# Projection products as four 32-column tiles between score visits that hold a value sum

## The chip, the core and the metric

The kernel runs on one core of one Trainium2 chip. The metric is the device time of one execution in microseconds (us). The core has a matrix engine (TensorE, PE in the profile; its weight loads are listed as PEld), a vector engine (VectorE, DVE), a scalar engine (ScalarE, ACT), a general engine (GpSimd, POOL) and an engine that here only issues DMAs (SyncE, SP). TensorE writes to PSUM, a memory of banks of 128 partitions x 512 float32.

## The reference

Two attention layers over 2,048 tokens, model width 640, 32 heads of 20, bfloat16; their outputs stand side by side.

```
A (memory-augmented, 4 segments of L = 512):
  q, k, v = x @ wq, x @ wk, x @ wv             per head, per segment s
  a_dot = softmax(q k^T / sqrt(20) + mask) v   inside the segment; the mask adds -1e9 where key > query
  a_mem = phi(q) M / (phi(q) z + 1e-6)         phi(t) = t + 1 if t > 0 else exp(t)
  o     = g * a_mem + (1 - g) * a_dot          g = sigmoid(beta) per head
  M    += phi(k)^T v ;  z += sum phi(k)        after the segment
  out_A = o @ wo
B (sliding window of 256):
  q, k, v = x @ wqkv
  out_B = softmax(q k^T / sqrt(20), where 0 <= query - key < 256) v @ wo
out = concat(out_A, out_B)
```

## The kernel before

The work is cut into eight chunks of 512 tokens that alternate, A0, B0, A1, B1 and so on to B3. For each chunk TensorE does three kinds of work, and each kind uses its array in another way, called a mode here:

- **Scores** (`score_batch`, line 745): four heads at once, each on 20 rows of the array (mode "row", or "row64" where only 64 keys are taken). One such batch is a *score visit*; there are 153. A visit fills two score tiles (`sc`, three buffers of two PSUM banks); ScalarE turns each into probabilities by an exponential (`pt`, line 761), and GpSimd (line 800) or VectorE (line 778) masks them.
- **Value sums** (`av`, line 814, and `av_tile`, line 835, for the last chunk): probabilities times values, four heads at once, each on 32 columns of the array and 32 PSUM partitions (mode "col"). Afterwards VectorE transposes (line 870) and GpSimd normalises (line 905).
- **Products** (`wide`, line 857): the q, k and v projections, the output projections, and the memory read `mem`, all on the whole array (mode "full"). There are 1,073 of them; most are part of a sum of five into one of the two PSUM banks `m0` and `m1`, which VectorE then copies out (lines 488, 664, 1014).

Nothing is scheduled on the chip: the order of all engines is written out while the kernel is built. `body` walks a planner's clock (`Flow`): `f.pe`, `f.act` and so on are the times at which the planner thinks each engine is free, and `on_pe` adds 97 ns whenever the mode changes. At each step `body` tries, in this order, a score visit (if its buffers and its q and k are there, and `may_wait` does not put it off), then the first entry of the list `pend` of due value sums and memory reads, then the first job that is ready among `jobs` (projections of the next chunk) and `fins` (output projections). A job yields between matmuls, so score visits may fall inside a sum of five. When all visits are out (`all_scored`), output projections use the score tiles instead of `m0` and `m1`, and the copy out of PSUM goes to ScalarE or VectorE, whichever the planner thinks is free; `last_job` and `last_half` finish the last 128 tokens.

`may_wait` is where `LEAD` acts:

```
if f.pe + LEAD > f.act:
    return False
```

It answers whether a score visit that could go may be put off; `f.act` is the planned end of ScalarE's queue.

`room` holds a score visit of 64-key tiles or a value sum back where many matmuls were issued in the last 3,000 planned ns; `on_pe` books each matmul for it through its argument `n`.

Of the kernel before, what the change touches and what calls it, by code (L numbers as in the profile page):

```python
# [13 lines left out]
P = 128  # L14
# [3 lines left out]
HD = 32  # L18
# [32 lines left out]
PATIENCE = 5000.0  # L51
LANES = 8
AHEAD = 100.0
LEAD = 500.0

def at_head(h):
    return VS * h + 12 * (h // 16)
# [1 line left out]
def mm_ns(n):  # L59
    return max(27.0, n / 2.4 + 2.5)  # L60

def whole(times):

    got = [t for ts in times for t in ts]
    return None if None in got else max(got)
# [147 lines left out]
class _K:  # L213
# [27 lines left out]
        self.f.bank_free[i] = t  # L241

    def warm_up(self, z):

        f = self.f
        ps, bi = self.bank()
        f.pe = max(f.pe, 1500.0)
        while f.pe + 700.0 < max(self.done[(0, "x", 0)], self.done[("wk_A", 0)]):
            self.wide(ps, z[:, 0:P], z[:, 0:L], L, True, True)
            f.flush()  # L250
        self.close(bi, f.seen)
# [602 lines left out]

    def wide(self, ps, lhsT, rhs, n, start, stop):

        self.nc.tensor.matmul(ps[:, 0:n], lhsT=lhsT, rhs=rhs, start=start, stop=stop)  # L857
        self.f.on_pe("full", mm_ns(n), n)
        self.f.left = 0 if stop else self.KT - 1 if start else self.f.left - 1

    def turn(self, O, bi):

        f = self.f
        while self.ring("tt", NTT) is None:
            if f.idle_dve:
                f.idle_dve.pop(0)[1]()
            else:
                heapq.heappop(f.later)[2]()
        tt, slot = self.piece("tt", NTT, 1, F32)
        self.nc.vector.transpose(out=tt[:], in_=O[:, :])  # L870
        t = f.on_dve(640.0, max(f.seen, slot["free"]))
        self.close(bi, t)
        return tt, slot, t
# [279 lines left out]
    def may_wait(self):  # L1153


        f = self.f
        if f.pe + LEAD > f.act:
            return False
# [56 lines left out]
    def body(self, xA, A_wq, A_wk, A_wv, A_wo, A_beta, xB, B_wqkv, B_wo, out2d):  # L1215
        nc, D, KT, f = self.nc, self.D, self.KT, self.f
# [89 lines left out]
        for m in range(KT):  # L1306
            first("k", m, self.kA, pk0)
            first("q", m, self.qA, None)
            v = lambda half: self.v_job(0, half, self.wv_A, self.vA, True,
                                        [self.known(0, "x"), self.known("wv_A", half)])  # L1310
# [5 lines left out]

        bs = self.batches(chunks)
        free_after = {}
        pend = []
        parts = {}  # L1320
        left = {}
        o_t = {}
        groups_done = {n: 0 for n in range(NC)}
# [3 lines left out]
        while True:  # L1327
# [3 lines left out]
            if i < len(bs):  # L1331
                n, ent, ms, complete = bs[i]
                kind, c = chunks[n]
                if self.ring("pt", NPT) is not None:
# [4 lines left out]
                    if None not in need:  # L1339
                        t = max(need + [f.room(4 * len(ent)) if ent[0][1][0] in "lust" else 0.0])  # L1340
# [21 lines left out]
            if pend:  # L1362
                n, g, what = pend[0]
                kind, c = chunks[n]
                if what == "tile":
                    ps_ = [p for x in range(4) for p in parts[(n, g[1] + x)]
                           if p[1] // P == g[0]]
                    need = [whole(p[6] for p in ps_), self.done.get((n, "v", g[1]))]
                elif what == "av":
                    ps_ = parts[(n, g)]  # L1370
# [4 lines left out]
                if None not in need and not (f.open and 0 < f.left <= 3):  # L1375
                    t = max(need + [min(f.bank_free), f.room(
                        4 * len(ps_)) if what != "mem" else 0.0])
# [9 lines left out]
            for x, jb in enumerate(self.jobs + self.fins):  # L1387
                if f.open and not jb[0] is self.opener:
                    continue
                t = self.need_time(jb[1])  # L1390
# [191 lines left out]
```

## Time and profile before

| what | before |
|---|---|
| median of 3 runs | 334.92 us (334.56 to 336.06) |
| profiled execution, time | 334.66 us |
| profiled execution, span | 332.9 us |
| TensorE busy | 317.7 us (95%), 6,617 matmuls and as many weight loads |
| ScalarE busy | 302.4 us (91%) |
| VectorE / GpSimd busy | 266.0 us (80%) / 255.7 us (77%) |
| granted TensorE clock | 1.00 |
| instruction queue q8 | 51 packets, 0.84 MB |

The span runs from the first to the last instruction of the program; the execution's own time lies 1.76 us above it. Busy times are unions of the recorded instructions of an engine. Matmuls are pipelined and the ends of their records are modelled, so a record of 300 ns can stand 137 ns behind the one before it; how long a product occupies the array is read from the distance of the starts. In a list of waits, "issue" means that an engine waited for nothing that the profile shows.

### The profile page before, as it was taken

The numbers are of one execution on the slowest core, as the hardware profiler recorded it, in microseconds if no ns is written. First come the engines' busy times: TensorE is split into PE (matmuls) and PEld (weight loads), VectorE is DVE, ScalarE is ACT, GpSimd is POOL, SyncE is SP. The second block draws the span as 40 slices with busy tenths as digits, with TensorE's granted clock in tenths as the row PEclk, the third lists the DMA queues.
The fourth block names the chain that finished last, engine by engine and source line by source line (L and its number), as shares of the span: only waits on it lengthen the run. The fifth ranks groups of instructions, "written<-read, shape, count | busy, mean of one in ns | idle before, by whom it ended". The sixth has DMA issues, their size and how long they took to land.

```text
span 332.9 us, 15825 instructions
## 1 busy us (share of the span) xinstructions
PE 317.7 (95%) x6617; PEld 174.1 (52%) x6617; DVE 266.0 (80%) x556; ACT 302.4 (91%) x332; POOL 255.7 (77%) x648
## 2 busy tenths in 40 slices
PE   7999999999999999999999999999999999999996
PEld 2444446554444455546654546455654545666564
DVE  6878667788988899989958898888677898876653
ACT  1879999998999999999999999989999999999841
POOL 8446779987668799984876879996965969977750
PEclk9999999999999999999999999999999999999999
DMA  6975745846566852245699245044584054659762
GB/s 195 397 245 135 194 134 121 177 117 183 127 207 145 182 147 75 47 98 107 167 209 189 65 90 161 2 98 69 136 168 114 14 161 126 154 135 192 169 138 99
DMA packets 76260, 47.36 MB, mean 142 GB/s; under 512 B 48381, under 2 KB 73181, under 8 KB 76189
## 3 DMA queue, kind: packets, MB, share of 16 engines
q1 hardware_dynamic: 75469, 45.71, 56.2%
q8 instruction: 51, 0.84, 1.0%
q10 hardware_dynamic: 720, 0.66, 0.7%
q14 instruction: 20, 0.16, 0.2%
HBM read 17.62 MB, written 16.96 MB: 104 GB/s over the span
## 4 chain that ended last, share of the span: by engine, by line
PE 56%; DVE 16%; ACT 11%; POOL 7%; issue 6%; DMA 2%; SPq 1%; ACTq 0%; DVEq 0%; POOLq 0%
PE m L857 35%; PE sc L745 11%; ACT pt L761 11%; PE m L814 6%; POOL pt L800 4%; DVE pt L778 3%; PE m L835 2%; POOL u L905 2%; DVE tt L870 2%; DVE kA L488 2%; DVE pq L529 2%; DMA beta<-in_A_beta_dram 1%; DVE vA L664 1%; DVE pq L523 1%; DVE ot L1014 1%
## 5 line engine op out<-in xcount | busy, mean ns | idle before, releaser
L761 ACT ACTIVATE pt<-sc 128x1024 bf16<-128x1024 f32 (+2 forms) x306 | 284.8, 1014 | 12.4 <-PE sc L745 10.0
L800 POOL TENSOR_SCALAR_AFFINE_SELECT pt<-pt 128x128 bf16<-128x128 bf16 (+1 forms) x512 | 176.7, 373 | 62.1 <-ACT pt L761 58.4
L870 DVE STREAM_TRANSPOSE tt<-m 128x512 f32<-128x512 f32 x88 | 61.4, 711 | 20.3 <-PE m L814 9.6
L905 POOL TENSOR_TENSOR o<-tt,rr 128x320 bf16<-128x320 f32 x64 | 47.6, 743 | 4.4 <-DVE rr L895 4.1
L857 PEld LDWEIGHTS <-xT 128*128 128x128 bf16 x350 | 32.0, 97 | 25.0 <-issue 13.3
L745 PE MATMUL sc<-qB,kB 20*64 20x64 bf16 (+2 forms) x1728 | 38.6, 218 | 1.2 <-issue 0.7
L778 DVE TENSOR_TENSOR pt<-pt,ends 128x1024 bf16<-128x1024 bf16 (+2 forms) x50 | 36.0, 734 | 0.0
L745 PEld LDWEIGHTS <-kB 20*64 20x64 bf16 (+1 forms) x1728 | 21.6, 98 | 23.3 <-issue 22.0
L745 PE MATMUL sc<-qA,kA 20*64 20x64 bf16 (+4 forms) x1024 | 33.3, 237 | 0.4 <-ACT qA L485 0.2
L1014 DVE CAST ot<-m 128x320 bf16<-128x320 f32 x56 | 26.8, 485 | 7.5 <-PE m L857 7.3
L857 PEld LDWEIGHTS <-oT 128*128 128x128 bf16 x280 | 24.7, 98 | 11.4 <-issue 1.0
L857 PE MATMUL m<-wBv,xT 128*128 128x320 bf16 x160 | 27.0, 299 | 2.4 <-DVE tt L870 2.3
L857 PE MATMUL m<-wv_A,xT 128*128 128x320 bf16 x160 | 26.1, 299 | 2.6 <-DVE vA L664 1.9
L857 PE MATMUL m<-xT,wq_A 128*128 128x512 bf16 x100 | 25.8, 380 | 1.5 <-DVE vA L664 1.0
L857 PE MATMUL m<-xT,wk_A 128*128 128x512 bf16 x100 | 26.0, 388 | 1.1 <-DVE qA L488 0.7
L857 PE MATMUL m<-xT,wBq 128*128 128x512 bf16 x100 | 26.8, 381 | 0.1
L857 PE MATMUL m<-xT,wBk 128*128 128x512 bf16 x100 | 25.9, 381 | 0.0
L745 PEld LDWEIGHTS <-kA 20*128 20x128 bf16 (+1 forms) x1024 | 13.6, 97 | 20.8 <-issue 19.8
L814 PE MATMUL m<-pt,vA 128*32 128x192 bf16 (+3 forms) x512 | 23.7, 275 | 0.0
L857 PE MATMUL m<-wo_A,oT 128*128 128x320 bf16 x140 | 22.7, 300 | 0.2
L488 DVE CAST kB<-m 128x512 bf16<-128x512 f32 x20 | 13.8, 691 | 9.2 <-PE m L857 9.2
L857 PE MATMUL m<-wo_B,oT 128*128 128x320 bf16 x120 | 19.4, 300 | 0.3 <-DVE ot L1014 0.3
(108 smaller groups left out, 405.9 us busy)
## 6 DMA issues: line engine op xcount, KB each, us to landing
out_dram<-ot SPq DMA_DIRECT2D x29, 160.0 KB
scr_o<-o SPq DMA_DIRECT2D x28, 160.0 KB
xT<-in_B_x_dram SPq DMA_DIRECT2D x8, 288.0 KB
xT<-in_A_x_dram SPq DMA_DIRECT2D x8, 256.0 KB
scr_pk<-e SPq DMA_DIRECT2D x15, 128.0 KB
vS<-vA SPq DMA_DIRECT2D x16, 87.0 KB
vL<-vB SPq DMA_DIRECT2D x8, 174.0 KB
scr_kA<-kA SPq DMA_DIRECT2D x16, 60.0 KB
```

What stands on the lines that cost most here:

```text
L488: nc.vector.tensor_copy(out=dst[:, m, at:at + L], in_=ps[:, :])
L529: nc.vector.tensor_tensor(out=r if len(box) == 1 else e, in0=r, in1=e, op=ALU.min)
L745: nc.tensor.matmul(ps[j // 2][h0:h1, j % 2, c0:c0 + nq], lhsT=k[rows, g, k0:k0 + h1 - h0], rhs=q[rows, g, q0:q0 + nq], start=True, stop=Tr ...
L761: nc.scalar.activation(out=pt[:, :, lo:hi], in_=ps[i][:, :, lo:hi], func=ACT.Exp, scale=self.scale)
L778: nc.vector.tensor_tensor(out=blk, in0=blk, in1=self.ends[:, c0, :].unsqueeze(1).unsqueeze(1) .to_broadcast([P, 2, n // SH, SH]), op=ALU.mult)
L800: nc.gpsimd.affine_select(out=blk, in_=blk, pattern=pat, compare_op=ALU.is_ge, fill=self.zero, base=base, channel_multiplier=mul)
L814: nc.tensor.matmul(O[HD * j:HD * j + HD, q0:q0 + nq], lhsT=v[:, at_head(h):at_head(h) + HD], rhs=pts[j // 2][:, j % 2, c0:c0 + nq], start= ...
L835: nc.tensor.matmul(O[HD * j:HD * j + HD, o0:o0 + nq], lhsT=v[:, at_head(h):at_head(h) + HD], rhs=pts[j // 2][:, j % 2, c0:c0 + nq], start= ...
L857: self.nc.tensor.matmul(ps[:, 0:n], lhsT=lhsT, rhs=rhs, start=start, stop=stop)
L870: self.nc.vector.transpose(out=tt[:], in_=O[:, :])
L905: nc.gpsimd.tensor_tensor(out=to[:] if add_to else to, in0=a, in1=b, op=ALU.mult)
L1014: nc.vector.tensor_copy(out=ot[:, 320 * hf:320 * hf + 320], in_=ps[:, 0:320])
```

## The change

`wide` now has two forms. In the new one a product is written as four matmuls on 32 columns each, in the mode of the value sums, and the planner books the mode "col" for it. It is taken in two cases: the planner's mode is already "col" and the next due value sum is not of the last chunk (or none is due); or the mode is not "full" and a value sum falls due soon (`sums_soon`: within the first `PEEK` = 2 entries of `pend`, memory reads skipped, a value sum whose probabilities and values are planned to be there within `SOON` = 700 ns; none for the last chunk). Otherwise the product goes over the whole array as before. `LEAD` goes from 500 to 800. `pend` and `parts` become attributes so that `wide` can see them.

```diff
-LEAD = 500.0
+LEAD = 800.0
+COL_NS = 3.0
+SOON = 700.0
+PEEK = 2
...
     def wide(self, ps, lhsT, rhs, n, start, stop):
 
-        self.nc.tensor.matmul(ps[:, 0:n], lhsT=lhsT, rhs=rhs, start=start, stop=stop)
-        self.f.on_pe("full", mm_ns(n), n)
+        f = self.f
+        if f.mode == "col" and not (self.pend and self.pend[0][0] == len(self.chunks) - 1) or f.mode != "full" and self.sums_soon():
+            for j in range(4):
+                s = slice(HD * j, HD * j + HD)
+                self.nc.tensor.matmul(ps[s, 0:n], lhsT=lhsT[:, s], rhs=rhs, start=start,
+                                      stop=stop, tile_position=(0, HD * j),
+                                      skip_group_check=True)
+            f.on_pe("col", n / 2.4 + COL_NS, n, 0.0, 4)
+        else:
+            self.nc.tensor.matmul(ps[:, 0:n], lhsT=lhsT, rhs=rhs, start=start, stop=stop,
+                                  skip_group_check=True)
+            f.on_pe("full", mm_ns(n), n)
         self.f.left = 0 if stop else self.KT - 1 if start else self.f.left - 1
+
+    def sums_soon(self):
+
+        f = self.f
+        if self.pend and self.pend[0][0] == len(self.chunks) - 1:
+            return False
+        for n, g, what in self.pend[:PEEK]:
+            if what == "mem":
+                continue
+            t = self.sums_need(n, g, what)
+            return t is not None and t <= f.pe + SOON
+        return False
+
+    def sums_need(self, n, g, what):
+        if what == "tile":
+            ps_ = [p for x in range(4) for p in self.parts[(n, g[1] + x)] if p[1] // P == g[0]]
+            t = self.done.get((n, "v", g[1]))
+        else:
+            ps_ = self.parts[(n, g)]
+            t = self.done.get((n, "v", g))
+        t0 = whole(p[6] for p in ps_)
+        return None if t is None or t0 is None else max(t, t0)
...
-        pend = []
-        parts = {}
+        self.pend = pend = []
+        self.parts = parts = {}
```

The prediction speaks of the order of the built program: the list of each engine's instructions as the kernel writes them out, which can be read without running it.

More of the change, by code (lines that the diff above doesn't have):

```diff
@@ L243, in warm_up @@
     def warm_up(self, z):
+        self.pend = []
         f = self.f
```

## The prediction

> **What bounds the kernel now.** I read the page's busy times first, then the waits, then the busy time of each engine by chunk, then TensorE's timeline around single changes of array mode. From the page, each engine's busy time:
>
> ```profile
> PE 317.7 (95%) x6617; PEld 174.1 (52%) x6617; DVE 266.0 (80%) x556; ACT 302.4 (91%) x332; POOL 255.7 (77%) x648
> ```
>
> TensorE (PE) leads, ScalarE (ACT) is close. A busy PE includes the modelled ends of matmuls, so the share alone does not say which of the two sets the pace. The waits (engine and line, what it waited for: us in total, times, longest):
>
> ```profile
> PEld L745 <- issue: 41.8, 131, 0.9
> PEld L857 <- issue: 32.3, 121, 1.0
> ACT pt L761 <- PE sc L745: 10.0, 24, 1.5
> ```
>
> The first two are not waits for data: the next weight load sits behind a change between score, product and value-sum modes. The third is ACT starved of scores: 10.0 us in 24 places. Then stretches, each from one chunk's first score visit to the next chunk's, the last row after the final visit (length; busy time of PE, PEld, DVE, ACT, POOL with instruction counts; clock; DMA share; GB/s):
>
> ```profile
> 8.40:47.60 39.20, 38.43 (x597) 18.37 (x600) 29.20 (x59) 35.75 (x41) 22.65 (x70) 1.00 0.71 215
> 47.60:89.20 41.60, 39.97 (x881) 22.26 (x874) 34.19 (x68) 39.73 (x48) 35.34 (x82) 1.00 0.61 155
> 89.20:123.40 34.20, 33.35 (x621) 16.21 (x619) 29.34 (x69) 33.74 (x37) 27.35 (x76) 1.00 0.68 163
> 123.40:167.80 44.40, 42.25 (x982) 25.11 (x981) 40.66 (x83) 42.66 (x48) 37.34 (x81) 1.00 0.44 108
> 167.80:202.20 34.40, 33.54 (x633) 16.51 (x631) 27.95 (x64) 33.83 (x36) 26.68 (x76) 1.00 0.69 135
> 202.20:245.00 42.80, 40.88 (x972) 23.92 (x971) 35.18 (x71) 40.57 (x45) 36.93 (x81) 1.00 0.44 96
> 245.00:279.20 34.20, 33.36 (x633) 16.37 (x631) 28.04 (x64) 33.73 (x36) 26.55 (x76) 1.00 0.43 115
> 279.20:317.10 37.90, 36.63 (x1065) 24.34 (x1063) 28.70 (x62) 36.10 (x40) 31.24 (x74) 1.00 0.71 157
> 317.10:332.90 15.80, 12.61 (x235) 8.79 (x234) 7.38 (x15) 4.56 (x7) 4.43 (x10) 1.00 0.44 114
> ```
>
> ACT's idle time (length less ACT) is 3.45, 1.87, 0.46, 1.74, 0.57, 2.23, 0.47 and 1.80 us: 12.6 us before the final visit. In A chunks 2, 4 and 6 ACT is full, so a lighter PE gains little there. After the final visit PE works alone.
>
> **The price of a mode change.** TensorE's timeline (start us, us, engine, line, shape, count, idle):
>
> ```profile
> 308.91 1.53 PE L857 MATMUL m<-wo_B,oT 128*128 128x320 bf16 x10
> 310.38 0.40 PE L745 MATMUL sc<-qB,kB 20*128 20x128 bf16 x16
> 310.71 0.30 PE L835 MATMUL m<-pt,vB 128*32 128x128 bf16 x8
> ...
> 102.16 0.59 PE L814 MATMUL m<-pt,vA 128*32 128x448 bf16 x12
> 102.58 0.29 PE L814 MATMUL m<-pt,vS 128*32 128x64 bf16 x16
> 102.69 0.21 PE L814 MATMUL m<-pt,vA 128*32 128x64 bf16 x4
> ```
>
> Ten 320-column products last 1.53 us with a single one at 0.30 (page: 300 ns), so one starts every (1.53 - 0.30)/9 = 0.137 us, and the tenth stops streaming at 308.91 + 1.37 = 310.28. The score matmuls start at 310.38: 0.10 us lost. Those 16 go four at a time, four steps of about 0.055 us, done at 310.60; the value sums start at 310.71: 0.11 us. I take 97 ns a change, bounds 90 and 110.
>
> **The change, part by part.**
>
> *Fewer changes.* In the built order TensorE changes mode 382 times before and 324 times after; score visits stay at 153. Of the 62 stretches between visits that hold a value sum, 51 are now in column mode throughout. 58 x 97 ns = 5.6 us less on PE (5.2 to 6.4).
>
> *273 of 1,073 products as four tiles.* A product becomes four loads and four matmuls, 819 more of each. Its streaming time: the twelve 448-, 320- and 192-column matmuls (three steps, four at a time) fill 102.16 to 102.58, 0.42 us for 960 columns, or 0.44 ns a column; the product above has 0.137/320 = 0.43. So column mode streams at the same rate, and I take nothing for the 273. The trace has no product in this mode, so I keep the 0.01 ns between the two as the bound: 0.01 x 380 columns (their mean, about) x 273 = 1.0 us either way.
>
> The four loads must hide. The sixteen 64-column matmuls start at 102.58 and the next group at 102.69: 0.11 us for four steps, each with four loads of mean 96 ns (row of L814's loads), 28 ns a step. So loads overlap the steps before them. [...]
>
> *More instructions to fetch.* The page's instruction queue q8 moved 51 packets, 0.84 MB (16 KB each), which fits TensorE's 13,234 loads and matmuls at 63 bytes; 1,638 more add 12%. What a shortage costs is seen perhaps once: eleven score matmuls at 315.41 stand 0.74 us behind "issue" after a burst of 64. I take nothing, bounds 0 and 4.7 us (6.4 more packets, 0.74 us each).
>
> *LEAD 500 to 800.* `may_wait` puts a score off only if ACT's queue reaches beyond `pe + LEAD`; a larger LEAD puts scores off less. The order shows it: products ahead of the final score visit fall from 174.9 to 169.8 us of streaming, and those behind it rise from 9.6 to 14.7. So 5.1 us move into the last stretch, where only PE works and is hardly idle until 329.8: all 5.1 us (0.6 either way) lengthen the tail. The short description of the change says the opposite of what the test does.
>
> *Moved copies.* Four more 640-column copies go from VectorE (DVE, two of 485 ns) to ACT, in the tail, where ACT is busy 4.56 of 15.80 us. Each takes about 0.69 us beside 1.37 us of products; nothing. Four output stores and some DMA issues swap queue with them; they land beside work, except the last one, which ends the span as now.
>
> *What is late next.* Before the final visit PE has 10.7 us less to do (5.6 + 5.1). It can bring that visit forward only as far as ACT has idle time to give. By chunk, PE's work in the order (columns plus 97 ns a change) falls by 0.7, 2.1, 1.6, 0.3, 2.1, 0.9, 2.1 and 0.9 us. Taking the smaller of that and ACT's idle: 0.7 + 1.9 + 0.5 + 0.3 + 0.6 + 0.9 + 0.5 + 0.9 = 6.3. Chunks 2, 4 and 6 leave 4 us unused; PE may carry a lead over into the next chunk, but three score tiles hold only half a visit beyond the one being read, about one exponential (1,014 ns). So 0 to 1 us at each of three borders; I take half, 1.5. Sum: 7.8 us (6.3 to 9.3).
>
> Total: 5.1 - 7.8 = -2.7, less nothing else. The profiled execution took 334.66 us (span 332.9, 1.76 around it), giving 332.0; the median shown, 334.92, is 0.26 above it. I round the gain to 2.5: **332.4 us**. A measurement of this kernel can tell about 0.5% (1.7 us) from no change.
>
> **Rivals.**
>
> 1. *PE alone sets the end* (0.18). 95% busy speaks for it, the full ACT in chunks 2, 4 and 6 against. All 5.6 us show: 329.3.
> 2. *ACT cannot come earlier* (0.22), slower. In the B chunks its idle may end with a query or key copied by DVE (busy 40.66 of 44.40 us in chunk 3), not with a freer PE. Then LEAD has moved 5.1 us into the tail and gets less back. It decides below 5.1 us of ACT idle recovered; at 3 us the time is 334.9 + 2.1 = 337.0. For it: the smallest fall in PE work is where DVE is fullest. Against: the waits name PE for 10.0 us of ACT's idle.
> 3. *Instruction fetch* (0.07): 4.7 us of stalls against a gain of 2.5, 337.1. Against: stretches of 64 score matmuls and value sums already run denser than any product in four tiles.
> 4. *Loads do not hide* (0.03): one load (97 ns) exposed per product, 273 x 97 ns = 26.5 us, about 359. The 28 ns step speaks against.
> 5. *It does not do what it says*: the mode changes do go (order), the "put off" does not; that is already in the sum.
>
> **How the numbers follow.** The forecast case (0.50) spans ACT recovering 6 to 9.3 us: 334.0 to 330.7. About 0.3 of it lies over 1.7 us below today, 0.2 within. Rival 1 adds 0.18 to faster; rival 2 gives 0.16 to slower and 0.06 to same; rival 3 splits 0.06 to slower and 0.01 to same; rival 4 is slower. Faster 0.48, same 0.27, slower 0.25. The range runs from rival 1 (329.3, less 0.3 for the upper price of a change) to rival 2's 337.0, leaving out rival 4 and the far side of rivals 2 and 3.
>
> **What would show it.** After: "issue" waits of the weight loads down by about 58 places; four-tile products of 320 columns starting 0.137 us apart; ACT's wait for scores down from 10.0 us to some 3 to 4; the final score visit near 309.3 instead of 317.15; then 17 to 18 us of tail in place of 12.6 of PE work. If the final visit is later than 312, rival 2 holds; if the 320-column step exceeds 0.15 us, rival 4; new "issue" gaps within a mode, rival 3. A time outside 329 to 337 would make the sum wrong altogether.

## The result, and the profile after

The changed kernel takes 339.88 us (median of 17 runs, 336.21 to 341.62); before takes 334.68 (17 runs, 333.98 to 336.06). The ratio is 1.0138, 95% interval 1.0115 to 1.0161: **slower by 1.4%**, where 0.7% faster was forecast. (The ratio compares the mean times, without the run of 341.62 us, which fell in a slower state of the chip.) The profiled execution took 339.30 us, span 337.6, against 334.66 and 332.9: 4.6 to 4.7 us longer.

Busy times of the engines, page of the changed kernel:

```profile
PE 313.6 (93%) x7401; PEld 177.7 (53%) x7436; DVE 263.8 (78%) x548; ACT 301.3 (89%) x336; POOL 254.8 (75%) x648
```

TensorE (PE) is less busy than before (313.6 against 317.7 us) in a longer span. (35 matmul records are missing here; each can look like a short gap.) The waits:

```profile
PEld L750 <- issue: 42.7, 127, 1.3
PEld L871 <- issue: 24.0, 76, 1.9
PEld L866 <- issue: 11.6, 46, 1.1
ACT pt L766 <- PE sc L750: 11.6, 22, 1.7
PE sc L750 <- issue: 2.7, 2, 1.5
PE m L819 <- POOL pt L805: 2.0, 3, 0.7
```

ScalarE (ACT) is starved of scores for 11.6 us, not less than the 10.0 before. The last two lines are new in size: score matmuls stopped behind no data for 2.7 us (0.7 before), and value sums waited 2.0 us for GpSimd's masks. Then the same stretches as in the prediction, from one chunk's first score visit to the next, the last one after the final visit:

```profile
8.00:47.80 39.80, 37.63 (x675) 19.06 (x684) 29.51 (x59) 35.62 (x42) 23.58 (x71) 1.00 0.69 213
47.80:87.80 40.00, 37.53 (x931) 21.90 (x933) 33.35 (x64) 38.45 (x46) 34.13 (x81) 1.00 0.59 154
87.80:122.00 34.20, 31.70 (x687) 16.07 (x683) 29.55 (x68) 33.63 (x38) 26.73 (x75) 1.00 0.71 152
122.00:166.90 44.90, 41.84 (x1072) 25.90 (x1071) 40.11 (x84) 42.49 (x48) 37.61 (x81) 1.00 0.48 122
166.90:201.30 34.40, 31.79 (x696) 15.68 (x695) 27.19 (x61) 32.87 (x37) 26.77 (x77) 1.00 0.56 118
201.30:243.90 42.60, 40.05 (x1049) 23.94 (x1050) 35.16 (x70) 40.49 (x44) 36.60 (x80) 1.00 0.38 88
243.90:276.70 32.80, 31.61 (x698) 15.60 (x695) 27.57 (x61) 32.79 (x37) 26.89 (x77) 1.00 0.44 103
276.70:315.80 39.10, 36.87 (x1087) 24.01 (x1080) 28.29 (x60) 35.76 (x39) 31.09 (x73) 1.00 0.75 163
315.80:337.60 21.80, 18.23 (x544) 13.37 (x542) 7.81 (x16) 7.62 (x12) 4.58 (x10) 1.00 0.51 137
```

Two rows carry the loss. The last stretch is 21.8 us instead of 15.8, with 18.23 us of PE instead of 12.61: the products that LEAD moved. (Its border lies 0.36 us ahead of the final visit here; from the visit itself it is 21.4 us against 15.8.) The stretches before it hardly shrank: the last chunk begins 2.5 us earlier (276.7 against 279.2), then takes 39.1 us instead of 37.9, so the final visit comes only 1.0 us earlier (316.16 against 317.15). ACT's idle before it, length less ACT over the first eight rows, is 15.7 us instead of 12.6. The trace of this execution has no record of the granted clock, so the 1.00 in its rows is not measured; but nowhere in it do products of 320 columns follow each other 0.27 us apart, as they do inside the half-clock window of the run with tiles alone below.

The last chunk loses its lead at one place. Its second score visit starts 2.2 us earlier than before (279.18 against 281.38), its third only 0.7 us (282.21 against 282.88). In both kernels a value sum and a product of the memory read stand between these two visits; in the changed order seven output products have come in as well, and they wait for a transpose:

```profile
281.15 1.14 PE L866 MATMUL m<-wo_A,oT 128*32 128x320 bf16 x28 [0.34 <-DVE tt L907]
282.21 1.29 PE L750 MATMUL sc<-qB,kB 20*64 20x64 bf16 x64
```

ScalarE then idles for 1.70 us, its longest wait for scores in this execution.

A product in four tiles costs what was forecast. TensorE's timeline, ten products of 320 columns as 40 matmuls:

```profile
320.50 1.53 PE L866 MATMUL sc<-wo_B,oT 128*32 128x320 bf16 x40
321.86 1.12 PE L866 MATMUL sc<-wo_A,oT 128*32 128x320 bf16 x28
```

(1.53 - 0.30)/9 = 0.137 us apart, the same as on the whole array, and the next group starts 1.36 us on. Counted in the trace, mode changes are 382 before and 324 after. Two stalls stand out, both inside one mode:

```profile
172.89 0.39 PE L750 MATMUL sc<-qA,kA 20*128 20x448 bf16 x7
174.81 0.18 PE L750 MATMUL sc<-qA,kA 20*128 20x64 bf16 x1 [1.52 <-issue]
...
313.10 0.23 PE L750 MATMUL sc<-qB,kB 20*128 20x128 bf16 x4
314.49 0.35 PE L750 MATMUL sc<-qB,kB 20*128 20x128 bf16 x12 [1.15 <-issue]
```

Score matmuls that wait for no semaphore start 1.52 and 1.15 us late. The DMA records have a 16 KB packet of the instruction queue q8 landing 1.43 and 1.52 us before (at 173.37 and 312.97). In the kernel before, the one such stall (0.74 us, at 315.41) ended 1.33 us after a packet (314.08).

### The profile page after: what moved, and what is told of

The parts are those of the page before. It is cut to its first block, busy times and chain, and to the rows that moved or that the text cites. A ratio compares the mean times of both kernels' runs of the same rounds, so it can differ in the third digit from the quotient of the medians.

```text
span 337.6 us, 17420 instructions
## 1 busy us (share of the span) xinstructions
PE 313.6 (93%) x7401; PEld 177.7 (53%) x7436; DVE 263.8 (78%) x548; ACT 301.3 (89%) x336; POOL 254.8 (75%) x648
## 4 chain that ended last, share of the span: by engine, by line
PE 30%; DVE 11%; ACT 6%; issue 5%; POOL 2%; DMA 2%; SPq 1%; ACTq 0%; DVEq 0%; POOLq 0%
PE m L871 12%; ACT pt L766 6%; PE sc L750 5%; PE m L866 5%; PE m L819 3%; DVE tt L907 3%; PE sc L866 2%; PE m L840 2%; POOL pt L805 2%; DVE pt L783 1%; DMA qB<-scr_qB 1%; DVE ot L1051 1%; DVE pq L534 1%; DVE kA L493 1%; DVE qB L493 1%
## 5 line engine op out<-in xcount | busy, mean ns | idle before, releaser
L766 ACT ACTIVATE pt<-sc 128x1024 bf16<-128x1024 f32 (+2 forms) x306 | 281.3, 1034 | 14.2 <-PE sc L750 11.6
L783 DVE TENSOR_TENSOR pt<-pt,ends 128x1024 bf16<-128x1024 bf16 (+2 forms) x50 | 37.9, 767 | 0.0
L871 PEld LDWEIGHTS <-xT 128*128 128x128 bf16 x275 | 24.9, 97 | 18.9 <-issue 8.9
L1051 DVE CAST ot<-m 128x320 bf16<-128x320 f32 x48 | 23.3, 485 | 11.4 <-PE m L871 8.3
L871 PE MATMUL m<-wBv,xT 128*128 128x320 bf16 x135 | 21.9, 299 | 1.2 <-DVE vB L674 0.6
L871 PEld LDWEIGHTS <-oT 128*128 128x128 bf16 x198 | 17.2, 98 | 8.7 <-issue 1.1
L871 PE MATMUL m<-xT,wBk 128*128 128x512 bf16 x72 | 20.4, 380 | 1.2 <-issue 0.6
L871 PE MATMUL m<-xT,wq_A 128*128 128x512 bf16 x67 | 18.1, 380 | 1.5 <-DVE vA L669 0.5
L493 DVE CAST qB<-m 128x512 bf16<-128x512 f32 x20 | 13.8, 689 | 7.2 <-PE m L866 6.6
L674 DVE CAST vB<-m 128x320 bf16<-128x320 f32 x32 | 15.1, 472 | 4.1 <-PE m L866 1.6
L942 POOL TENSOR_TENSOR u<-tt,rr 128x320 bf16<-128x320 f32 x24 | 17.4, 724 | 0.4 <-DVE rr L930 0.4
```

Source lines behind the costliest of these rows:

```text
L493: nc.vector.tensor_copy(out=dst[:, m, at:at + L], in_=ps[:, :])
L674: nc.vector.tensor_copy(out=dst, in_=src)
L766: nc.scalar.activation(out=pt[:, :, lo:hi], in_=ps[i][:, :, lo:hi], func=ACT.Exp, scale=self.scale)
L783: nc.vector.tensor_tensor(out=blk, in0=blk, in1=self.ends[:, c0, :].unsqueeze(1).unsqueeze(1) .to_broadcast([P, 2, n // SH, SH]), op=ALU.mult)
L942: nc.gpsimd.tensor_tensor(out=to[:] if add_to else to, in0=a, in1=b, op=ALU.mult)
L1051: nc.vector.tensor_copy(out=ot[:, 320 * hf:320 * hf + 320], in_=ps[:, 0:320])
```

## The experiments

All are compared with before on the same chip, five rounds; the ratios are not those of the medians and can differ from them by a few tenths of a per cent. The expectations name theories T1 to T4, each explained where it first comes up. The three columns on the right come from one profiled execution of each kernel. "Lead at the last chunk" is how much earlier than before the first score visit of chunk B3 (the 134th) starts in the profiled execution; "final visit" likewise (+ is later); "tail" runs from the start of the final visit to the end of the last product's columns. "Quartered" products shift the places where instruction packets end (see below).

| kernel | ratio (95%) | lead at the last chunk, us | final visit, us | tail, us |
|---|---|---|---|---|
| before | 1 | 0 | 0 | 12.5 |
| changed | 1.0138 (1.0115 to 1.0161) | 2.5 | -1.0 | 18.1 |
| LEAD 800 alone | 1.0125 (1.0085 to 1.0165) | 5.9 | -3.2 | 19.1 |
| changed, LEAD 500 | 1.0308 (1.0286 to 1.0330) | -6.3 | +11.5 | 12.0 |
| tiles on the order of before | 1.0001 (0.9973 to 1.0030) | 2.5 | +0.4 | 12.5 |
| order of the changed kernel, whole products | 1.0209 (1.0183 to 1.0234) | 1.8 | +2.7 | 17.6 |
| tiles on the order of before, 21 quartered | 0.9995 (0.9973 to 1.0017) | 0.9 | -0.7 | 12.5 |
| before, 21 quartered | 1.0088 (1.0059 to 1.0117) | -1.6 | +4.2 | 12.5 |
| changed, LEAD 650 | 1.0136 (1.0101 to 1.0171) | 2.8 | +4.6 | 12.1 |
| LEAD 800 order, tiles | 1.0117 (1.0087 to 1.0147) | 4.6 | -1.8 | 18.7 |
| tiles on the order of before, 10 quartered | 0.9951 (0.9930 to 0.9971) | -0.5 | +0.1 | 12.5 |
| tiles on the order of before, 32 quartered | 0.9999 (0.9974 to 1.0024) | 0.0 | +2.6 | 12.5 |
| changed, 21 quartered | 1.0154 (1.0128 to 1.0180) | 3.0 | +1.3 | 18.5 |
| LEAD 800 alone, 21 quartered | 1.0127 (1.0093 to 1.0160) | | | |

**LEAD alone.** The kernel before with one constant changed:

```diff
-LEAD = 500.0
+LEAD = 800.0
```

> The kernel before with LEAD 800 instead of 500 and nothing else: no product in tiles. Its order on TensorE has 393 mode changes (before 382), and the products behind the last score visit rise from 9.6 to 16.0 us of streaming. Theory T1 (the 5 to 6 us that LEAD moves into the tail are the loss, because ScalarE cannot come forward): 4 to 6 us slower, last score visit about where it was. Theory T2 (the extra weight loads and matmuls run TensorE out of instructions, and scores come late): within 1.5 us of before, since it has no extra instruction. Theory T3 (a product in tiles costs more than a whole one): as before, within 1.5 us.

1.0125, T1's number; T2's and T3's "within 1.5 us" missed. The tail grew by 6.6 us, and the visits, 5.9 us ahead at the last chunk, kept 3.2 us at the end. The third visit of that chunk loses 1.6 us of the lead, as in the changed kernel (five output products stand ahead of it here). Then comes:

```profile
291.00 0.58 PE L857 MATMUL m<-wo_A,oT 128*128 128x320 bf16 x3 [1.98 <-issue]
```

with TensorE's clock at half from 291.6 to 295.0 us. So the tail (T1) is paid, but T1 was wrong that ScalarE cannot come forward: it came 5.9 us forward, and T2's stall appeared in a kernel without one extra instruction.

**Tiles with LEAD 500.** The changed kernel with the old constant.

```diff
-LEAD = 800.0
+LEAD = 500.0
```

> The changed kernel with LEAD back at 500: 234 products in tiles, 321 mode changes, and only 2.8 us of products behind the last score visit. T1: the tail's 5 us are gone, so faster than the changed kernel by 4 us or more, about 334 to 336. T2: the instructions are still there (702 more pairs), so 338 or more and still stalls without a semaphore of 3 to 5 us in all. T3: 338 or more, with the 320-column step in tiles above 0.15 us.

1.0308, a median of 345.48 us. T1's 334 to 336 is far off; T2's and T3's "338 or more" holds, but without their signs: score matmuls wait behind no semaphore for 2.0 us in all, not 3 to 5, and 320-column products in tiles start 0.136 us apart (median). The tail is 12.0 us, although only 2.8 us of products are in it: TensorE waits 2.90 us in it for a DMA (`xT<-scr_o`) and runs at half clock from 330.2 to 337.1 us. The final visit is 11.5 us late:

```profile
ACT pt L766 <- PE sc L750: 21.1, 27, 3.2
```

ACT starves for 21.1 us. The order shows that more scores are put off: products ahead of the final visit are 181.7 us, not 174.9. The reason is read from the code and not tested by itself: with tiles the planner books less time on TensorE, so ACT's planned queue looks longer, and `may_wait` puts a score off more often. LEAD 800 takes this back (169.8 us).

**Tiles alone.** The order of before, with 159 products (`TILES`: those between two visits with a value sum) written as tiles, in the form of the change; the planner is not told.

```diff
+        x = self.wide_n = getattr(self, "wide_n", -1) + 1
+        if x in TILES:
+            for j in range(4):
...
+        else:
             self.nc.tensor.matmul(ps[:, 0:n], lhsT=lhsT, rhs=rhs, start=start, stop=stop)
         self.f.on_pe("full", mm_ns(n), n)
```

> The order of the kernel before, instruction for instruction, but 159 products that stand between two score visits with a value sum are written as four tiles: 319 mode changes instead of 382, 477 more pairs, the tail as before. T1: TensorE has 6 us less to do and nothing moved, so 2 to 6 us faster. T2: stalls for instructions take it back, between 1 us faster and 3 us slower, with stalls without a semaphore well above the one of 0.9 us before. T3: 2 us slower or more.

1.0001. 319 mode changes make 6.1 us less work (63 fewer at 97 ns, an estimate); the visits are 2.5 us ahead at the last chunk. Then the lead is lost at one place:

```profile
291.79 0.45 PE L876 MATMUL m<-wo_B,oT 128*128 128x320 bf16 x2
293.91 1.74 PE L876 MATMUL m<-wo_B,oT 128*128 128x320 bf16 x8 [1.68 <-issue]
```

and in the page's row of TensorE's clock (tenths of full speed in 40 slices of the span):

```profile
PEclk9999999999999999999999999999999999979999
```

A stall of 1.68 us, and then a window of 3.41 us at half clock (the 7; 294.5 to 298.0 us), which costs another 1.7 us. The last chunk's instructions on TensorE are those of before, one for one, but for one memory-read product in tiles. Of its twelve timed runs those with a mean granted clock of 0.998 or more took 333.4 to 334.3 us, those at 0.995 took 334.9 to 335.9, those at 0.989 took 337.7 and 338.2: one or two such windows are the spread.

**Order alone.** The changed kernel's order, with whole products.

```diff
-            for j in range(4):
...
+            self.nc.tensor.matmul(ps[:, 0:n], lhsT=lhsT, rhs=rhs, start=start, stop=stop,
+                                  skip_group_check=True)
             f.on_pe("col", n / 2.4 + COL_NS, n, 0.0, 4)
```

> The order of the changed kernel, with every product on the whole array: 386 mode changes instead of 324, no extra instruction, 14.7 us of products in the tail. T1: the order is what costs, and the mode changes come back on top: 340 to 345 us. T2: without the extra instructions at most 2 us above before, and faster than the changed kernel. T3: faster than the changed kernel by more than 2 us, for all its mode changes.

1.0209, T1's number, but with a stall of 3.06 us at 296.67 and a half-clock window of 3.41 us behind it, in a kernel without extra instructions, which T1 did not ask for. Against LEAD alone it has nearly the same PE work ahead of the 134th visit (4.0 us and 4.2 us less than before), yet leads by 1.8 us instead of 5.9: the order that the planner makes when it reckons with tiles is worse on the chip. One sign of it is in its waits:

```profile
PE m L819 <- POOL pt L805: 2.1, 3, 0.7
```

2.1 us of value sums that wait for masks, as in the changed kernel (LEAD alone: 0.7).

**Half a packet more.** 21 early whole products are cut into four column quarters: 63 more loads and matmuls, 126 instructions, about 0.16 us of work by the planner's 2.5 ns a matmul (`mm_ns`).

```diff
+        if x in PAD:
+            for c in range(0, n, n // 4):
+                self.nc.tensor.matmul(ps[:, c:c + n // 4], lhsT=lhsT, rhs=rhs[:, c:c + n // 4],
+                                      start=start, stop=stop, skip_group_check=True)
```

This shifts all later packet ends by 126 instructions. On the tiles-alone kernel:

> The kernel with 159 products in tiles on the order of before (the form-only run), plus 21 early whole-array products cut into four column quarters each: 63 more pairs, 126 instructions, half a 16 KB instruction packet, 0.16 us of work. In the form-only run the score visits were 2.5 us ahead of before up to 291 us and then lost 3.9 us to one stall without a semaphore and the half-clock window behind it. Theory T2 (where a packet of instructions ends inside a burst decides the stall): the stall moves or goes; if it goes, 332 to 333 us, if it lands in another burst, 335 or more, but not the same stall at the same visit. T1 (ScalarE cannot use what TensorE saves): 334 to 335, as the form-only run.

0.9995, median 334.38. The stall at 293.91 is gone; others of 1.28 and 1.20 us stand at 172.09 and 313.04, so T2 is right on the place; its 335 or more for that case is a little too much, and the time is in T1's range. On the kernel before:

> The kernel before with the same 21 products cut into quarters and nothing else: half a packet more, no mode change removed. T2: the stall of 0.9 us at the last but one score visit moves or goes, so between 0.9 us faster and 4 us slower, and different in place. T1: 0.2 us slower, no more.

1.0088, 2.9 us for 0.16 us of work. The stall of before is gone and two stand elsewhere, one with a half-clock window behind it:

```profile
304.71 0.64 PE L747 MATMUL sc<-qB,kB 20*64 20x64 bf16 x56
306.83 0.24 PE L747 MATMUL sc<-qB,kB 20*64 20x64 bf16 x8 [1.49 <-issue]
```

Its page, the clock's row:

```profile
PEclk9999999999999999999999999999999999997999
```

The other is 1.16 us at 174.11. T2's prediction of place and size holds, T1's 0.2 us does not. This is the price of a shift in where the instruction packets end, with tail, order and modes untouched.

**LEAD 650.** The changed kernel with a tail as before:

```diff
-LEAD = 800.0
+LEAD = 650.0
```

> The changed kernel with LEAD 650: 251 products in tiles, 323 mode changes, 9.0 us of products behind the last score visit instead of 14.7 (before: 9.6). T1 (the tail is the loss): about 5 us faster than the changed kernel, 334 to 336. T4 (the order that the planner makes when it knows of the tiles makes score visits late: value sums wait for masks, scores are put off): the last score visit comes later by what the tail is shorter, 338 to 342.

1.0136. The tail is 12.1 us, and the final visit is 4.6 us late. That is T4's number, not T1's: what leaves the tail comes back ahead of the visits.

**Tiles on LEAD's own order.** 216 products in tiles, planner not told:

```diff
-LEAD = 500.0
+LEAD = 800.0
...
+        if x in TILES:
```

> The order of the LEAD-only run (planner unaware of tiles, LEAD 800), with 216 of its products between visits with a value sum written as tiles: 322 mode changes, 16.0 us of products in the tail. T4: without the planner's reordering, score visits stand 6 us or more ahead of before at 279 us (changed kernel: 2.5), and the time is 333 to 336. T1: the tail of 16 us costs as in the LEAD-only run, 337 to 339 whatever the form. T2: 335 to 341 depending on stalls in the last 40 us.

1.0117. The lead at the last chunk is 4.6 us, more than the changed kernel's 2.5, less than T4's 6; a stall of 1.73 us at 292.10 and a half-clock window from 293.5 took 3 us of it, and the third visit of that chunk 1.5 us. With a tail of 18.7 us, the time is T1's number. Against LEAD alone, 71 mode changes fewer gained next to nothing (1.0117 and 1.0125), and the lead at the last chunk is smaller (4.6 and 5.9).

**Other offsets.** Tiles alone with 10 and with 32 products quartered (`PAD` shorter and longer, else as above):

> The form-only kernel with 10 early products in quarters: 30 more pairs, a quarter of an instruction packet. T2 (packet ends decide the stalls): the visits are again 2 to 2.5 us ahead wherever no stall without a semaphore has come yet; 332 to 333 us if none comes in the last 160 us, 334 to 336 if one does. T1 (ScalarE cannot use what TensorE saves): 334 to 335.

> The form-only kernel with 32 early products in quarters: 96 more pairs, three quarters of a packet, 0.24 us of work. T2: as with 10, 332 to 333 without a stall, 334 to 336 with one; the four offsets (0, 10, 21, 32) differ by 1 us or more among themselves. T1: all four within 0.7 us.

0.9951 and 0.9999. With 10 the runs are 332.66 to 335.41 us, median 333.70 against 335.28: **faster than before by 0.5%**, the only kernel here that beats both. It is the best of four offsets, and nothing but the offset sets it apart. Its profiled execution (334.75 us) is one of its longer ones and shows that luck is not steady: stalls of 1.23 and 1.93 us at 27.43 and 173.87. With 32 the profiled execution (337.29 us) has a stall of 1.47 us at 305.26 and a half-clock window from 306.1. The ratios of the four offsets (0, 21, 10, 32) lie between 0.9951 and 1.0001 of before; T1's 0.7 us is exceeded.

**Offsets of the changed kernel and of LEAD alone.** The same 21 quarters, put into the whole-array branch of the changed kernel and into the LEAD-alone kernel.

> The changed kernel with 21 early whole products in quarters: half a packet more, the same order. T2: the stall of 1.7 us at 174.5 us and that of 1.3 us at 314.2 us move or go, and the time changes by 1 us or more either way (336 to 343). T1: the tail stays 18 us and the time 339 to 341, since the last score visit is bound by ScalarE and not by stalls.

> The LEAD-only kernel with 21 early products in quarters. In the LEAD-only run the visits stood 5.9 us ahead at 279 us and lost 3 us to a stall at 290.7 us and a half-clock window behind it. T2: with the stall elsewhere the last visit stands up to 5 us ahead of before and the time is 335.5 to 337; with a stall in the last 60 us, 338 or more. T1: 338 to 339 as before, for the tail of 19 us.

1.0154 and 1.0127. The changed kernel's stalls at 174.8 and 314.5 went, one of 1.36 us came at 297.73 and a half-clock window from 283.6 to 287.0, and the tail stayed at 18.5 us; the time did not leave T1's 339 to 341, and T2's change of 1 us or more did not come. Without the stall at 174.8 the lead at the last chunk is 3.0 us instead of 2.5. This offset brought neither of the two near before, so stalls alone do not explain their loss. LEAD alone again takes 1.3% longer than before; its profiled execution is its longest run (342.54 us) and is left out of the table. Its one run at a mean granted clock of 1.000 took 337.00 us, the others, at 0.995, 339.84 or more: there stalls and windows may be a good part of the loss, but one run does not show it.

## Why the prediction was wrong, step by step

**Fewer changes, and a tile's streaming: right.** 382 to 324 in the trace, and 0.137 us a product in either form. The loads stay hidden: the four tiles of a product take all 128 rows, one load has a mean of 96 ns (`<-oT`, line 866 of the changed kernel), and none of the four shows in the 0.137 us. The sign I named, about 58 fewer "issue" waits, failed: 279 places became 270. Those lines count idle stretches of PEld, not changes.

**LEAD's 5.1 us in the tail: right.** The tail grew by 5.6 us, of which a stall of 0.42 us at 323.9 is part.

**What is late next: the step that failed.** I let the final visit come 7.8 us forward; it came 1.0. The lead at the last chunk was 2.5 us where 5.4 without any carry were summed for the first seven chunks, and the last chunk lost 1.5 us where it should have won 0.9. That last loss falls where the seven products stand ahead of the chunk's third visit (1.06 us, and 0.34 us of waiting ahead of them); every kernel here with a LEAD of 650 or 800 loses 1.4 to 1.6 us there, in tiles or not, and none with 500 does, so it comes with LEAD's order. The carried 1.5 us had no support. The error was to bound PE's relief by ACT's idle and then to take all of that idle as recoverable, as if each visit would move up with PE's total. Visits stand in an order fixed ahead of time, and tiles on an unchanged order turned 6.0 us of relief into 2.5, with no stall ahead of the last chunk; at the three other offsets into 0.9, 0.0 and -0.5.

**The planner's order was taken as given.** I read from the order how much work stands before each visit, and not what each value sum then waits for. The order-alone run shows that this is worth 4.1 us of lead against LEAD alone at the same work (a stall of 0.74 us at 172.71 in the one is part of it). Which of its differences does it, beyond the 2.1 us of masks, stays open.

**Instruction supply: the term that was mis-sized at nothing.** I gave it 0 to 4.7 us and tied it to the number of instructions. It depends on where packets end: 126 instructions cost the kernel before 2.9 us, and kernels with no extra instruction (LEAD alone, order alone) stall for 1.98 and 3.06 us. In the changed kernel, the stalls of 1.52 and 1.15 us ahead of the final visit compare with 0.74 before; in the profiled execution the first seems to cost 0.5 us of lead (2.5 against 3.0 without it) and the second 0.3 us against the stall of before, an estimate of under 1 us together from these leads. The same order offset by half a packet was no faster. So in this kernel the term is small beside the 6.8 us by which the final visit is late.

**The rivals.** Rival 2 described the outcome (a final visit later than 312, a longer tail not paid back) but its reason was wrong: with LEAD alone ACT did come 5.9 us forward, so a limit by DVE's copies did not stop it there. Rival 3 was a real mechanism under the wrong rule, rival 4 is refuted, and rival 1 did not show. That the scores are put off for more products is true after all of the tiles, as the run with LEAD 500 shows; LEAD 800 counters it.

## What to carry to other kernels

Time saved on the busiest engine is worth what the second engine can start earlier in the order as written (here 2.5 us of lead for 6.0 us of relief, with tiles alone); compare that order alone, without the saving, before adding the saving up. A change that moves work behind the last dependent step pays for it in full (here 5.1 us moved, and the tail 5.6 us longer), while its return has to survive every stall before. On a kernel whose TensorE stream has bursts of small matmuls, a shift of half an instruction packet that adds next to no work is a control worth running: it moved this kernel by 0.9%, where the change under study moved it by 1.4%.

## What the runs showed of the hardware

TensorE's instructions come in packets of 16 KB (queue q8: 51 before, 58 after). The profiled executions in the table (all but the last row) have 19 stalls of 0.7 to 3.06 us behind no semaphore. Each ends 1.26 to 1.53 us after a q8 packet landed. Each also stands at the same place in the instruction stream: the weight loads issued by then (351 at the earliest, 6,876 at the latest), divided by 128, leave 91 to 95, and the quotient is the number of packets landed in the trace by then (before: 6,364 loads and 49 packets; changed: 3,548 and 27, 6,876 and 53). As every load has one matmul, 128 loads are 256 instructions, which at 16 KB is 64 bytes each; over the whole kernel before it is 63 (51 packets, 13,234 loads and matmuls). My reading is that in these dense stretches TensorE ran up to the end of what had landed. No execution has more than two such stalls at its 51 to 58 packet ends; at the others no stall of that size is seen. Which ends stall is not worked out in general.

Six of the 19 stalls (1.47 to 3.06 us) were followed by one window at half the granted clock. In tiles alone, products of 320 columns start 0.27 us apart in it instead of 0.137. It lasted 3.41 us in tiles alone and in order alone, longer than the stalls before it (1.68 and 3.06 us); in tiles alone the pair cost 3.9 us. Two stalls of that size, 1.52 us (changed, where no products 0.27 us apart follow) and 1.93 us (10 quartered), came without a window, and one window, in the changed kernel with 21 quartered, came with no stall of 0.7 us near it. What sets the clock down is not shown.
